# The tail of a one-core transformer block: residual through an identity matmul, W1 over both tiles at once, last copies on two engines

## The chip, the cores and the metric

The kernel runs on one core of one Trainium2 chip. The metric is the device time of one execution in microseconds (us). The engines are PE (TensorE, with its weight load PEld), DVE (VectorE), ACT (ScalarE), POOL (GpSimd) and SP (SyncE, which issues nearly all DMAs). Each works through its own instructions in the order in which the program lists them, and waits for the others through semaphores.

## The reference

One transformer block with adaptive layer norm: 2048 tokens, width 512, 32 heads of 16, an MLP of 1376. The vector c gives six modulation vectors of 512 (sa, ca, ga, sb, cb, gb).

```python
mod = (_silu(c) @ w_mod).reshape(c.shape[0], 6, 1, -1)
sa, ca, ga, sb, cb, gb = (mod[:, 0].copy(), mod[:, 1].copy(), mod[:, 2].copy(),
                          mod[:, 3].copy(), mod[:, 4].copy(), mod[:, 5].copy())
h = _layernorm(x, axis=-1) * (1 + ca) + sa
x = x + ga * _A_ref(h, A_wqkv, A_wo)      # softmax attention, 32 heads of 16, then wo
h = _layernorm(x, axis=-1) * (1 + cb) + sb
x = x + gb * _B_ref(h, B_w1, B_b1, B_w2, B_b2)   # gelu(h @ w1 + b1) @ w2 + b2
```

The gates ga and gb are multiplied into Wo and W2 once, so that a residual is a plain sum.

## The kernel before, in words

The tokens are four blocks of 512 queries (QB); a block is four tiles of 128 tokens (P). A run is one block with four heads: 32 runs, over 16 key tiles each. For a key tile PE computes the transposed scores (L822), an engine takes the exponential, and PE multiplies by V (L960), where one more column of V collects the softmax denominators, into a bank `od`.

The exponential is taken in two ways. ACT takes scores of two or three heads at a time (L871, 128x1024 or 128x1536). Of each run up to four key tiles are offered to DVE (125 in all): it converts scores to integers (L912) and adds four shifts (L927), and PE sums five weighted pieces. ACT takes over such a tile when it has no own one left, so the split follows the order of work.

All other work lies between these: projections, layer norms, and, for each finished block, `block_tail`: W_o and the residual (L1166), layer norm, W1 (L1183), GELU (L1202) and W2 (L1123, L1214).

No engine order is written by hand. The class `Plan` simulates the engines with a fixed cost for every operation while the program is built and always issues the operation that can start first; ties are broken by priorities and by a pseudo-random term, `spread`: SPREAD times a hash of the operation's kind or source line and of one of 32 SEEDS, one for each 25 us. `heat` adds dummy matmuls on PE (L431, L436, L447): PE work within the last WIN = 3.4 us of planned time is summed, and while it is under HEAT, dummy work may go in.

The last block is done in halves, so that its first half (tiles 0 and 1) can be finished under the last attention runs. Its tail, `block_tail(LAST, 2)`, is called after run 27; it loads the whole block's x (512 KB) into `xr`, adds the W_o product of tiles 0 and 1 to it in place (`x2 = xr`), and computes W1 with 256 columns in 11 groups of 128 rows of F. Eight of them (PSUM_F = 8) go through DVE into `g` (L1193), three wait until the attention's banks are free (L1189). GELU needs another ACT table than the exponential, so it and W2 come after the last exponential.

What is left then is `last_half` (L1223 to L1315), tiles 2 and 3. Its steps in before:

- L1226 loads x of the last block a second time. SP issues in order; ahead of it stand the four copies of L1022, which shift the upper half of run 30's product to its place and wait for POOL (L1012).
- L1237 (`early`): W_o over three of the four head groups, which do not need the last run, for both tiles.
- For each tile on DVE: transpose of its half of `od` (L1249), reciprocal of the denominators (L1251), transpose back as a broadcast (L1253), product (L1256). `s` ties the second tile's chain behind the first tile's statistics.
- L1263 (`wo2`): the last head group's W_o, two matmuls. L1267: the residual add on DVE. L1270: statistics; L1271: reciprocal root on POOL; L1272: normalise.
- L1283: four transposes on PE; L1287: modulate, two on DVE and two on ACT.
- L1295: W1 over 128 columns, 44 matmuls for a tile; L1298: GELU, 11 for a tile; L1305 (which prints as L1123): W2, 11 matmuls of 512 columns; L1310: second residual on DVE; L1313: the output DMA.

After the attention, the five banks of the scores become five banks `t` (`r_t`) for these steps; two banks `ax` (`r_ax`) hold W2 of the first half.

Of the kernel before, what the change touches and what calls it, by code (L numbers as in the profile page):

```python
# [11 lines left out]
ACT = mybir.ActivationFunctionType  # L12
ALU = mybir.AluOpType
ENG = mybir.EngineType
BF16 = mybir.dt.bfloat16
FP32 = mybir.dt.float32
# [37 lines left out]
PEL = 0.24  # L54
# [3 lines left out]
DPL = 0.08  # L58
AL = 0.17
FILL = 1.6  # L60
SPREAD = 0.15
SEEDS = (571, 338, 517, 702, 966, 607, 659, 937, 623, 185, 209, 513, 12, 512, 674, 785, 660, 579, 642, 245, 112, 195, 497, 319, 388, 80, 556, 716, 338, 990, 290, 195)
HEAT = 1.3


class Res:
# [191 lines left out]
def kernel(  # L258
# [126 lines left out]
    def op(eng, *a, **k):  # L385
        o = Op(eng, *a, **k)
        if eng == "PE":
            o.due = due_now[0]
            due_now[0] += due_now[1]
        return plan.add(o)  # L390
# [98 lines left out]
    def load_x(b, deps=()):  # L489
        def go(o):  # L490
            nc.sync.dma_start(out=o.tile, in_=x_src[b])
        return dma(go, deps, kb=512, acq=r_xb, prio=0.0)
# [111 lines left out]
    def stats(ln, t, src):  # L604
        mv, _ = ln.tile
        st6 = work.tile([P, 6], FP32, name="ln_s", bufs=2)
        nc.vector.bn_stats(out=st6, in_=src)  # L607
        nc.vector.bn_aggr(out=mv[:, t, :], in_=st6)
# [7 lines left out]
    def apply(ln, z, t, src):  # L616
        mv, rs = ln.tile
        nc.vector.tensor_scalar(out=z.tile[:, t, :], in0=src, scalar1=mv[:, t, 0:1],
                                scalar2=rs[:, t:t + 1], op0=ALU.subtract, op1=ALU.mult)
# [9 lines left out]
    def copy(eng, dst, src):  # L629
        if eng == "ACT":  # L630
            nc.scalar.copy(out=dst, in_=src)
        else:
            nc.vector.tensor_copy(out=dst, in_=src)  # L633
# [480 lines left out]
    def wo_mm(ps, b, t, lo, hi):  # L1114
        for u in range(lo, hi):
            ot, at = (o_OT[(b, (t // 2) * NC + u)], (t % 2) * P) if b == LAST else (o_OT[(b, u)], t * P)
            nc.tensor.matmul(out=ps, lhsT=ot.tile[:, at:at + P], rhs=Wo[:, u, :],
                             start=(u == 0), stop=(u == NC - 1))
# [7 lines left out]
    def rows(f):  # L1126
        return P if f < NF - 1 else FL
# [25 lines left out]
    def block_tail(b, nt=TPB):  # L1153
        kind = "tail"
        due(prog() + 15, (TAIL if b < LAST - 1 else TAIL2 if b < LAST else TAIL3) / (9 * nt - 1))
        N = nt * P
        xr = load_x(b)
        x2 = xr
        ots = [o_OT[(b, u)] for u in range(NC)]
        res_done = []  # L1160
# [62 lines left out]
    def last_half():  # L1223
        r, b = NR - 1, LAST
        full = ("full", 0)
        xr = load_x(b)  # L1226

        def take(acq, deps=()):
            return op("NIL", None, 0.0, deps, lat=0.0, prio=0.0, acq=acq)
        x2 = xr  # L1230
        ln, z, h = take(r_ln, (x2,)), take(r_z, (x2,)), take(r_blk, (x2,))
        g = o_late["part"]
        od, OD, OT = o_od[r], take(r_OD), take(r_OT)
        o_OT[(b, 7)] = OT
        tiles = (2, 3)
        acc = {t: take(r_t) for t in tiles}
        early = {t: op("PE", lambda o, t=t: wo_mm(acc[t].tile, b, t, 0, 3), 3 * MM,  # L1237
                       [acc[t]] + [x for u in range(NC, 7) for x in o_OT[(b, u)].two], lat=PEL, mode=full,
                       kind="last", prio=0.5) for t in tiles}
        s = None  # L1240
        for n, t in enumerate(tiles):
            den = work.tile([P, 8], FP32, name=f"den{t}")

            def half(x, t=t):
                return x.rearrange("p (a q) -> p a q", a=2)[:, :, (t % 2) * P:(t % 2 + 1) * P]

            def turned(n):
                return OD.tile[:, n * HB:(n + 1) * HB].rearrange("p (a q) -> p a q", a=2)
            sh = op("DVE", lambda o, t=t, half=half: nc.vector.transpose(out=turned(0), in_=half(od.tile)), 0.35,  # L1249
                    (o_last[r], OD, s), prio=0.06 + n)  # L1250
            rc = op("DVE", lambda o, den=den: nc.vector.reciprocal(  # L1251
                out=den, in_=OD.tile[:, 16:HB:32]), 0.12, (sh,), prio=0.05 + n)
            bk = op("DVE", lambda o, den=den: nc.vector.transpose(  # L1253
                out=turned(1).rearrange("p a q -> p (a q)"),
                in_=den.unsqueeze(2).to_broadcast([P, 8, 32])), 0.35, (rc,), prio=0.045 + n)
            ml = [op("DVE", lambda o, t=t, half=half: nc.vector.tensor_tensor(  # L1256
                out=half(OT.tile), in0=half(od.tile), in1=turned(1), op=ALU.mult),
                0.36, (bk, OT), prio=0.04 + n)]

            def wo2(o, t=t):  # L1260
                for p in range(2):
                    at = p * HB + (t % 2) * P
                    nc.tensor.matmul(out=acc[t].tile, lhsT=OT.tile[:, at:at + P], rhs=WoP[:, p, :], start=False,  # L1263
                                     stop=(p == 1))
            w = op("PE", wo2, 2 * MM,
                   ml + [early[t]], lat=PEL, mode=full, kind="last", prio=0.2)
            a = op("DVE", lambda o, t=t: nc.vector.tensor_tensor(  # L1267
                out=x2.tile[:, t, :], in0=acc[t].tile, in1=xr.tile[:, t, :], op=ALU.add), 0.62,
                (w, x2, xr), prio=0.024 + n / 50, rel=(acc[t],))
            s = op("DVE", lambda o, t=t: stats(ln, t, x2.tile[:, t, :]), 0.83, (a, ln), prio=0.022 + n / 50)  # L1270
            rs = op("POOL", lambda o, t=t: rstd(ln, t, t + 1), 0.9, (s,), prio=0.0)  # L1271
            za = op("DVE", lambda o, t=t: apply(ln, z, t, x2.tile[:, t, :]), 0.33, (rs, z),  # L1272
                    prio=0.021 + n / 50)

            at = slice((t - 2) * P, (t - 1) * P)
            hd = []
            for e in ("DVE", "ACT"):
                js = (0, 1) if e == "DVE" else (2, 3)

                def tr(o, t=t, js=js):  # L1280
                    o.ps = o.tile.bitcast(BF16)[:, 0:2 * P]
                    for n, j in enumerate(js):
                        nc.tensor.transpose(out=o.ps[:, n * P:(n + 1) * P],  # L1283
                                            in_=z.tile[:, t, j * P:(j + 1) * P], identity=ident)
                tro = op("PE", tr, 2 * 0.0705, (za,), lat=PEL, mode=full, kind="last", acq=r_t, prio=0.1)
                for n, j in enumerate(js):
                    hd.append(op(e, lambda o, n=n, j=j, e=e, at=at, tro=tro: modulate(  # L1287
                        e, h.tile[:, j, at], tro.ps[:, n * P:(n + 1) * P], modB, j), 0.25, (tro, h),
                        prio=0.02, rel=(tro,)))
            gs = slice(HB + (t - 2) * P, HB + (t - 1) * P)  # L1290
            gd = []
            for f in range(NF):
                def w1(o, f=f, at=at):
                    for j in range(NC):
                        nc.tensor.matmul(out=o.tile[:, 0:P], lhsT=W1[:, j, f * P:(f + 1) * P],  # L1295
                                         rhs=h.tile[:, j, at], start=(j == 0), stop=(j == NC - 1))
                mm = op("PE", w1, 4 * 0.071, hd, lat=PEL, mode=full, kind="last", acq=r_t, prio=0.3)
                gd.append(op("ACT", lambda o, f=f, mm=mm, gs=gs: nc.scalar.activation(  # L1298
                    out=g.tile[0:rows(f), f, gs], in_=mm.tile[0:rows(f), 0:P], func=ACT.Gelu_apprx_tanh,
                    bias=b1c[0:rows(f), f:f + 1], scale=1.0), 0.25, (mm,), prio=0.3, rel=(mm,)))  # L1300
            first = prev = None
            for f in range(NF):
                def w2(o, f=f, gs=gs):
                    w2_mm((first_of[id(o)] or o).tile, g.tile, gs.start, f, f + 1)
                o = op("PE", w2, MM, (gd[f], prev), lat=PEL if f == NF - 1 else 0.0, mode=full,  # L1305
                       kind="last", acq=r_t if f == 0 else None, prio=0.4)
                first_of[id(o)] = first
                first = first or o
                prev = o
            a = op("DVE", lambda o, t=t, first=first: nc.vector.tensor_tensor(  # L1310
                out=o.tile, in0=first.tile, in1=x2.tile[:, t, :], op=ALU.add), 0.66, (prev,), prio=0.1,
                acq=r_o, rel=(first,))
            dma(lambda o, t=t, a=a: nc.sync.dma_start(  # L1313
                out=out[0][b * QB + t * P:b * QB + (t + 1) * P, :], in_=a.tile), (a,), kb=128,
                rel=(a,))  # L1315

    first_of = {}

    prev_tr = after = None
    for b in range(NQ):  # L1320
# [132 lines left out]
```

## Time and profile before

| | us |
|---|---|
| median of 12 executions | 789.81 (786.45 to 795.9) |
| profiled execution | 791.02 |
| its span, first to last instruction | 789.2 |
| before the first exponential stretch, 0 to 20 | ACT busy 8.5 |
| attention stage, 20 to 764.6 | ACT busy 737.1, DVE 714.6, PE 704.7 |
| tail, 764.6 to 789.2 | 24.6 long; ACT busy 11.9, DVE 10.4, PE 19.6 |
| VectorE's share of the exponential | 476 score tiles of 128x512 (119 key tiles) |
| dummy matmuls within the attention (L447) | 116, four to a group |
| mean granted TensorE clock | 0.995 |

How to read it: the busy time of a matmul runs from its start to its modelled end, so neighbouring ones overlap, and PE's busy time is more than it can be at its peak. "ACT busy" over a stage says whether the stage is bound by ACT. The granted clock is the share of full speed that the throttle let PE run at; a short dip hardly shows in the mean. Lines of the chain of waits have a start, a length, and the work or queue that the end was waiting for in that stretch.

### The profile page before, as it was taken

What the parts mean: (1) busy time and instruction counts of PE and PEld (TensorE: products, weight loads), DVE (VectorE), ACT (ScalarE), POOL (GpSimd) and SP (SyncE); (2) the same over time, 40 slices, a digit from 0 to 9 for tenths busy, and PEclk for the clock granted to TensorE, in tenths of its full rate; (3) what the DMA queues carried; (4) which work ended last, traced back from release to release, by engine and by line L of the source; (5) the groups of instructions that cost most, each with busy time, mean ns of one, the idle gap of its engine ahead of it and who ended that gap; (6) DMA issues with size and microseconds to landing.
All of it is one profiled execution on the core that took longest, in us unless ns stands there. A gap on an engine that the chain in (4) does not pass through costs nothing.

```text
span 789.2 us, 20525 instructions
## 1 busy us (share of the span) xinstructions
PE 741.1 (94%) x8286; PEld 273.0 (35%) x8286; DVE 737.3 (93%) x1285; ACT 757.6 (96%) x683; POOL 125.4 (16%) x279
## 2 busy tenths in 40 slices
PE   8889999999999898999999999999999999999997
PEld 3433333233332222223232233322243444344454
DVE  6889988999999999999999999999899999999974
ACT  4999999999999999999999999999999999999993
POOL 6511124121134300100002001001000100100100
PEclk9999999999999999999999999999999999999999
DMA  6152001101020010001000110001010001101010
GB/s 214 30 136 89 18 23 46 23 16 22 7 73 22 25 42 23 19 22 28 22 23 18 30 34 21 12 17 32 23 57 21 23 18 33 29 20 28 18 44 28
DMA packets 39073, 28.22 MB, mean 36 GB/s; under 512 B 17957, under 2 KB 34374, under 8 KB 38978
## 3 DMA queue, kind: packets, MB, share of 16 engines
q1 hardware_dynamic: 38970, 26.91, 12.4%
q8 instruction: 65, 1.06, 0.6%
q14 instruction: 30, 0.25, 0.1%
q10 hardware_dynamic: 8, 0.00, 0.0%
HBM read 21.30 MB, written 2.61 MB: 30 GB/s over the span
## 4 chain that ended last, share of the span: by engine, by line
ACT 22%; PE 22%; DVE 12%; issue 7%; DMA 1%; SPq 0%; POOL 0%; POOLq 0%; DVEq 0%; ACTq 0%
ACT pt L871 21%; PE od L960 7%; PE st L822 6%; DVE sh L927 5%; DVE ph L912 4%; PE ax L1123 3%; PE ax L1183 2%; PE ax L822 1%; ACT g L1202 1%; DVE ln_s L607 1%; DVE xb L1166 1%; PE t L1123 1%; DMA xb<-in_A_x_dram 0%; DVE g L1193 0%; DVE OD L985 0%
## 5 line engine op out<-in xcount | busy, mean ns | idle before, releaser
L871 ACT ACTIVATE pt<-st 128x1536 bf16<-128x1536 f32 x629 | 715.7, 1302 | 7.2 <-PE ax L822 3.9
L912 DVE TENSOR_SCALAR ph<-ax 128x512 int16<-128x512 f32 x476 | 311.0, 681 | 13.4 <-PE ax L822 12.1
L927 DVE TENSOR_SCALAR sh<-ph 128x2048 int16<-128x2048 int16 x476 | 311.0, 692 | 2.6 <-PE od L960 2.3
L822 PE MATMUL st<-qm,kT 32*128 32x512 bf16 x1572 | 246.7, 383 | 21.3 <-ACT pt L871 17.2
L822 PE MATMUL ax<-qm,kT 32*128 32x512 bf16 x476 | 167.6, 380 | 8.5 <-DVE ph L912 6.2
L960 PE MATMUL od<-sh,VX 128*32 128x512 bf16 (+1 forms) x2400 | 168.6, 342 | 5.5 <-DVE sh L927 4.5
L822 PEld LDWEIGHTS <-kT 32*128 32x128 bf16 x2048 | 80.5, 91 | 239.3 <-issue 230.3
L960 PE MATMUL od<-pt,VEB 128*32 128x512 bf16 (+1 forms) x1960 | 144.8, 341 | 0.3 <-ACT pt L871 0.3
L960 PEld LDWEIGHTS <-VX 128*32 128x32 bf16 x2400 | 60.7, 95 | 88.3 <-issue 78.0
L960 PEld LDWEIGHTS <-VEB 128*32 128x32 bf16 x2560 | 63.0, 96 | 76.5 <-issue 64.6
L1012 POOL TENSOR_TENSOR OT<-OD,RB 128x256 bf16<-128x256 f32 x38 | 27.3, 729 | 317.3 <-DVE sh L927 200.5
L960 PE MATMUL od<-ph,VEB 128*32 128x512 bf16 (+1 forms) x600 | 48.2, 345 | 1.8 <-DVE OD L985 1.6
L1012 POOL TENSOR_TENSOR OS<-OD,RB 128x256 bf16<-128x256 f32 x24 | 17.2, 729 | 158.1 <-DVE sh L927 110.9
L1183 PE MATMUL ax<-blk,W 128*128 128x512 bf16 (+1 forms) x164 | 41.8, 361 | 0.5 <-DVE ph L912 0.2
L701 PE MATMUL ax<-blk,w 128*128 128x512 bf16 x124 | 36.5, 382 | 2.1 <-DVE blk L626 0.9
L756 POOL TENSOR_SCALAR VX<-VEB 128x128 bf16<-128x128 bf16 x64 | 23.2, 362 | 81.4 <-DVE VEB L633 77.6
L1123 PE MATMUL ax<-w,g 128*128 128x512 bf16 x112 | 30.4, 382 | 0.4 <-DVE ph L912 0.2
L1193 DVE TENSOR_SCALAR g<-ax,b1c 128x512 bf16<-128x512 f32 (+1 forms) x41 | 28.1, 691 | 1.0 <-PE ax L1183 0.7
L607 DVE BATCH_NORM_STATS2 ln_s<-xb 128x6 f32<-128x512 bf16 x32 | 21.6, 675 | 1.5 <-DMA xb<-in_A_x_dram 1.5
L1123 PEld LDWEIGHTS <-g 128*128 128x128 bf16 x176 | 14.0, 97 | 23.3 <-issue 12.7
L985 DVE COPY OD<-od 128x512 f32<-128x512 f32 x31 | 21.1, 680 | 0.9 <-issue 0.5
L1183 PEld LDWEIGHTS <-W 128*128 128x128 bf16 x176 | 14.0, 97 | 20.6 <-issue 14.9
(110 smaller groups left out, 371.2 us busy)
## 6 DMA issues: line engine op xcount, KB each, us to landing
RB<-rn SPq DMA_DIRECT2D x124, 64.0 KB
xb<-in_A_x_dram SPq DMA_DIRECT2D x8, 512.0 KB
out_dram<-o SPq DMA_DIRECT2D x16, 128.0 KB
qm<-qs SPq DMA_DIRECT2D x120, 16.0 KB
W<-in_B_w_dram SPq DMA_DIRECT2D x1, 1376.0 KB
w<-in_A_wqkv_dram SPq DMA_DIRECT2D x3, 384.0 KB
blk<-in_w_mod_dram SPq DMA_DIRECT2D x2, 512.0 KB
xb<-in_w_mod_dram SPq DMA_DIRECT2D x2, 512.0 KB
```

Source lines behind the costliest of these rows:

```text
L607: nc.vector.bn_stats(out=st6, in_=src)
L701: return chain([(lambda ps, j=j: nc.tensor.matmul(out=ps[:, 0:QB], lhsT=w.tile[:, j, cc * P:(cc + 1) * P], rhs=o_h[b].tile[:, j, :], start ...
L756: nc.gpsimd.tensor_scalar(out=v_cols(VX[(t, ph)])[:, 8 * cc:8 * cc + 8, 0:16], in0=v_cols(v_tile(t, 0))[:, 8 * cc:8 * cc + 8, 0:16], scala ...
L822: nc.tensor.matmul(out=o.tile[:, k * QB:(k + 1) * QB], lhsT=kT[cc][kb][rows, ko * P:(ko + 1) * P], rhs=qm.tile[rows, par, :] if hb is None ...
L871: nc.scalar.activation(out=e.tile[:, 0:len(got) * QB], in_=o.tile[:, 0:len(got) * QB], func=ACT.Exp, scale=ESC)
L912: nc.vector.tensor_scalar(out=ph.tile[:, o.row * QB:(o.row + 1) * QB], in0=o.tile, scalar1=PH_B, scalar2=0.0, op0=ALU.add, op1=ALU.max)
L927: sh = op("DVE", lambda o, j=j: nc.vector.tensor_scalar(out=o.tile, in0=first.tile, scalar1=PH_SH[j], scalar2=None, op0=ALU.add), 0.6, es, ...
L960: nc.tensor.matmul(out=o_od[r].tile[32 * i:32 * i + 32, n * HB:n * HB + w], lhsT=v_tile(kt, ph)[:, c0:c0 + 32], rhs=got[i][:, at:at + w], ...
L1012: two = beside(lambda c: nc.gpsimd.tensor_tensor(out=OT.tile[:, c], in0=OD.tile[:, c], in1=o5.tile[:, c], op=ALU.mult), (OT,), (OD, o5))
L1123: nc.tensor.matmul(out=ps, lhsT=g[:, f, col:col + P], rhs=rhs, start=(f == 0), stop=(f == NF - 1))
L1183: mm = chain([(lambda ps, f=f, j=j: nc.tensor.matmul(out=ps[:, 0:N], lhsT=W1[:, j, f * P:(f + 1) * P], rhs=h.tile[:, j, 0:N], start=(j == ...
L1193: ev.append(op("DVE", lambda o, f=f, mm=mm: nc.vector.tensor_scalar(out=g.tile[:, f, 0:N], in0=mm.tile[:, 0:N], scalar1=b1c[:, f:f + 1], s ...
```

## The change

- The tail's second load of x goes; the last block's tail keeps its `xr` for tiles 2 and 3.
- `early` adds x to the W_o bank by an identity matmul. The statistics read the bank; ACT copies it to `x2`; the residual add goes.
- The normalisation of `od` is done once over 512 columns, for both tiles.
- The modulates of both tiles are collected in one list, and W1 runs once over 256 columns, with 11 GELUs of 256 columns.
- W2 of a tile begins with an identity matmul of x2; its end is copied out in two halves, one on DVE and one on ACT.
- HEAT goes from 1.3 to 1.4, SPREAD from 0.15 to 0.06, and all 32 SEEDS are other ones.

```diff
-SPREAD = 0.15
-SEEDS = (571, 338, 517, 702, ...)
-HEAT = 1.3
+SPREAD = 0.06
+SEEDS = (109, 104, 232, 177, ...)
+HEAT = 1.4
...
         xr = load_x(b)
+        if b == LAST:
+            xr.uses += 1
+            o_late["x"] = xr
...
-        xr = load_x(b)
+        xr = o_late["x"]
...
+        def begin(o, t):
+            wo_mm(acc[t].tile, b, t, 0, 3)
+            nc.tensor.matmul(out=acc[t].tile, lhsT=ident, rhs=xr.tile[:, t, :], start=False, stop=False)
+        early = {t: op("PE", lambda o, t=t: begin(o, t), 4 * MM,
+                       [acc[t], xr] + [x for u in range(NC, 7) for x in o_OT[(b, u)].two], lat=PEL, mode=full,
                        kind="last", prio=0.5) for t in tiles}
...
+        sh = op("DVE", lambda o: nc.vector.transpose(out=OD.tile, in_=od.tile), 0.6, (o_last[r], OD), prio=0.06)
+        rc = op("DVE", lambda o: nc.vector.reciprocal(out=den, in_=OD.tile[:, 16:QB:32]), 0.12, (sh,), prio=0.05)
+        bk = op("DVE", lambda o: nc.vector.transpose(
+            out=RB.tile, in_=den.unsqueeze(2).to_broadcast([P, 16, 32])), 0.6, (rc, RB), prio=0.045)
+        ml = [op("DVE", lambda o: nc.vector.tensor_tensor(
+            out=OT.tile, in0=od.tile, in1=RB.tile, op=ALU.mult), 0.62, (bk, OT), prio=0.04)]
+        hd, copies = [], {}
...
-            a = op("DVE", lambda o, t=t: nc.vector.tensor_tensor(
-                out=x2.tile[:, t, :], in0=acc[t].tile, in1=xr.tile[:, t, :], op=ALU.add), 0.62,
-                (w, x2, xr), prio=0.024 + n / 50, rel=(acc[t],))
-            s = op("DVE", lambda o, t=t: stats(ln, t, x2.tile[:, t, :]), 0.83, (a, ln), prio=0.022 + n / 50)
+            s = op("DVE", lambda o, t=t: stats(ln, t, acc[t].tile), 0.86, (w, ln), prio=0.022 + n / 50,
+                   rel=(acc[t],))
+            a = op("ACT", lambda o, t=t: nc.scalar.copy(out=x2.tile[:, t, :], in_=acc[t].tile), 0.5,
+                   (w, x2), lat=0.15, prio=0.02 + n / 50, rel=(acc[t],))
+            copies[t] = a
...
-            za = op("DVE", lambda o, t=t: apply(ln, z, t, x2.tile[:, t, :]), 0.33, (rs, z),
+            za = op("DVE", lambda o, t=t: apply(ln, z, t, x2.tile[:, t, :]), 0.33, (rs, z, a),
...
+        gd = []
+        for f in range(NF):
+            def w1(o, f=f):
+                for j in range(NC):
+                    nc.tensor.matmul(out=o.tile[:, 0:HB], lhsT=W1[:, j, f * P:(f + 1) * P],
+                                     rhs=h.tile[:, j, 0:HB], start=(j == 0), stop=(j == NC - 1))
+            mm = op("PE", w1, 4 * 0.12, hd, lat=PEL, mode=full, kind="last", acq=r_t, prio=0.3)
+            gd.append(op("ACT", lambda o, f=f, mm=mm: nc.scalar.activation(
+                out=g.tile[0:rows(f), f, HB:QB], in_=mm.tile[0:rows(f), 0:HB], func=ACT.Gelu_apprx_tanh,
+                bias=b1c[0:rows(f), f:f + 1], scale=1.0), 0.36, (mm,), prio=0.3, rel=(mm,)))
+        for t in tiles:
...
+            first = op("PE", lambda o, t=t: nc.tensor.matmul(
+                out=o.tile, lhsT=ident, rhs=x2.tile[:, t, :], start=True, stop=False), MM, (copies[t],),
+                mode=full, kind="last", acq=r_t, prio=0.4)
...
-            a = op("DVE", lambda o, t=t, first=first: nc.vector.tensor_tensor(
-                out=o.tile, in0=first.tile, in1=x2.tile[:, t, :], op=ALU.add), 0.66, (prev,), prio=0.1,
-                acq=r_o, rel=(first,))
+            o2 = take(r_o, (gd[NF - 1],))
+            a = [op(e, lambda o, e=e, cs=cs, first=first, o2=o2: copy(e, o2.tile[:, cs], first.tile[:, cs]), us,
+                    (prev, o2), prio=0.1, rel=(first,))
+                 for e, cs, us in (("DVE", slice(0, HB), 0.35), ("ACT", slice(HB, D), 0.32))]
```

## What I predict

> **What bounds the kernel now.** I read the page first, then the windows by stage, the chain of waits over the last 25 us, and last the PE timeline there. The first two say where 97% of the time lies:
>
> ```profile
> L871 ACT ACTIVATE pt<-st 128x1536 bf16<-128x1536 f32 x629 | 715.7, 1302 | 7.2 <-PE ax L822 3.9
> ```
> ```profile
> 20.00:764.60 744.60, 704.70 (x8001) 253.55 (x8001) 714.56 (x1228) 737.10 (x642) 110.55 (x224) 1.00 0.12 31
> ```
>
> The columns of the second are length, then busy time (and count) of PE, PEld, DVE, ACT, POOL, then granted clock. From 20 to 764.6 us ScalarE is busy 737.1 of 744.6 us: the attention stage is bound by the exponentials, and a new order can recover at most 7.5 us of idle ScalarE there, plus work passed to VectorE (30 us idle). Asked in 10 us pieces, two carry 2.7 of the 7.5 us, and 1 us pieces show why:
>
> ```profile
> 130.00:140.00 10.00, 9.86 (x95) 2.64 (x87) 6.84 (x12) 8.76 (x9) 6.09 (x10) 0.84 0.03 7
> ...
> 131.00:132.00 1.00, 1.00 (x12) 0.17 (x4) 0.00 (x0) 0.68 (x1) 1.00 (x2) 0.50 0.00 0
> ...
> 745.00:750.00 5.00, 4.91 (x79) 2.38 (x68) 3.58 (x6) 3.52 (x5) 0.00 (x0) 0.73 0.03 5
> ...
> 746.00:747.00 1.00, 1.00 (x20) 0.36 (x12) 0.17 (x1) 0.00 (x0) 0.00 (x0) 0.50 0.00 0
> ```
>
> The clock falls to 0.50 for about 3.4 us, twice; PE is late with the scores, and ScalarE and VectorE stand. After 764.6 us comes the tail, 24.6 us, where the chain of waits reads (start, length, what):
>
> ```profile
> 766.25 3.94 DMA xb<-in_A_x_dram
> ...
> 770.32 0.70 DVE xb L1267
> ...
> 775.45 0.70 DVE xb L1267
> ...
> 779.83 2.64 PE t L1295 x44
> 782.47 3.25 PE t L1123 x15
> ...
> 785.80 0.69 DVE o L1310
> ```
>
> A late load of x holds the first residual add to 770.32; the second tile's add follows 5.1 us later, as the DVE chain of tile 3 starts only after the statistics of tile 2. But the PE timeline shows what PE does meanwhile:
>
> ```profile
> 768.76 1.46 PE L1123 MATMUL ax<-w,g 128*128 128x512 bf16 x6
> ...
> 770.70 1.67 PE L1123 MATMUL ax<-w,g 128*128 128x512 bf16 x7
> 773.43 0.40 PE L1283 MATMUL t<-ident,z 128*128 128x128 bf16 x4 [1.05 <-DVE z L618]
> ...
> 778.57 0.40 PE L1283 MATMUL t<-ident,z 128*128 128x128 bf16 x4 [0.27 <-DVE z L618]
> ```
>
> It works off W2 of the first half. From 764.95 to 785.53 (start of the last W2 matmul, 785.31, plus one step) it has about 18.6 us of issue time and 1.96 us of holes (0.30 for the GELU at 766.3, 1.23 at 772.2, 0.43 at 778.1). So PE is the tail's real bound, and the DMA wait is mostly hidden.
>
> **What the skill says.** "TensorE: Matmul & The Clock Gate", section "Back-to-back issue gap", prices a step at columns/2.4 + 2.5 ns, 216 ns for 512. The trace agrees: three W2 matmuls take 0.81, less the last one's 0.379, over 2: 0.2155 us; 256 columns 0.110, 128 columns 0.058. The same page, "Part 1: The HAM clock gate", has the array half-clocked after an idle window of about 3.4 us, a window running freely; the trace shows 0.50 for that long, though PE was not idle by its busy row. "VectorE: DVE Perf Modes", section on the TRN2 errata, gives (N+151)/0.96 ns for an fp32 tensor_tensor: 691 at 512 (trace: 692), 424 at 256 (trace: 419). "ScalarE: Activation LUTs", "What ACT_TABLE_LOAD costs", has 280+0.833N ns with a pointer bias and 93 ns of overlap: 400 for 256 columns, where three L1189 GELUs took 1.18 us.
>
> **The change part by part.** Times below run on the profiled execution, 791.02 us, of which the span is 789.2; the median of the runs shown is 1.2 lower, 789.81, and I carry the differences over to it.
>
> *Load.* The second load of x (512 KB, one SP issue, 766.25 to 770.19) goes; tiles 2 and 3 of the load that the block already had (issued at 668.3) are used. Nothing else on SP follows until the outputs at 772.9. Late next is not the load but the W_o product: its third matmul waits for the shifts of run 30 (L1022, issued 763.79 to 766.2), and in before W_o and WoP run 767.01 to 768.75.
>
> *Normalisation over 512 columns, once.* Before, a half took 765.12 to 766.74 (0.45+0.20+0.45+0.42 and gaps). Now two transposes of 512 columns, for which no row exists: between 0.45 (fixed cost dominant) and 0.90 (twice); the 0.96 GHz slope of the errata section adds 0.27, so I take 0.70. With reciprocal 0.20, product 0.69 and four gaps: 2.4, ready at 767.5. That is 0.8 later for tile 2, but covered: WoP cannot issue before 768.3 anyway. With 0.90 it would be 767.9, still covered. Tile 3's own chain (1.45 us of DVE between 771.9 and 774.8) disappears.
>
> *Residual on PE.* Two identity matmuls join the early W_o: +0.43 us. W_o, identity and WoP for both tiles run 767.01 to 769.6. The adds L1267 (0.69 each) go; statistics read PSUM directly (0.69, or up to 0.1 more from PSUM). Two ScalarE copies of 0.63 (as the 128x512 CAST) come in at 769.4, where ScalarE idles 4.89 us; the normalise op waits for them, but they end at 770.7, before the reciprocal roots are there (1.02 after the statistics: 771.3). Nothing else is queued behind them until the modulates.
>
> *One chain for both tiles.* Statistics 769.4 to 770.3 and to 771.2; POOL 0.9 each; normalise 771.3 and 772.25; four transposes each; modulates 0.60 on DVE and 0.81 on ACT per tile, the last at about 774.0. So h of both tiles is complete where before tile 2 alone was (774.5); tile 3's came at 779.6.
>
> *W1 over 256 columns.* 44 matmuls at 0.110 for 88 at 0.058: 4.84 against 5.10, −0.26. GELU: 11 at 0.39 for 22 at 0.265, −1.5 us of ScalarE, which kept up before and does so now (0.39 against PE's 0.44 a group). The added wait for all eight modulates stands at the head of PE's queue; behind it W2 of the first half (22×0.2155 = 4.74) is what PE can do first. It fits: 769.6 + 20×0.2155 + two sets of transposes 0.48 = 774.4.
>
> *Last residual and copies.* Two more identity matmuls, +0.43. L1310 (0.69) becomes half on DVE (0.42) and half on ACT (128x256 without a bias: 0.40 to 0.46): −0.23. The output DMAs are the same, 2.7 us from the last write to the end.
>
> *Sum of the tail.* PE work 18.6 + 0.43 + 0.43 − 0.26 = 19.2, holes 1.96 down to about 0.45: PE ends 764.95 + 19.2 + 0.45 = 784.6 instead of 785.53, −0.9; copies −0.23. Tail: −1.15. No holes at all would give −1.6, today's holes +0.4.
>
> *"Eight early W1 groups".* PSUM_F is 8 in both; no line of the diff changes it. Nothing.
>
> *Constants of the planner.* SPREAD, SEEDS and HEAT reorder the whole program. HEAT 1.4 asks for more PE work in each window before dummy matmuls (29 groups now, L447) stop, so it bears on the two half-clock stretches: ScalarE lost 1.24 + 1.41 = 2.65 us in them. The cost is more filler at 0.2155 a step. If both stretches go, −2.65, with 0.3 given back: −2.3. Bounds: −7.5 (all idle) and, upward, the split of the work: VectorE does 119 tiles (476/4) of the 125 that the code offers it; each tile more on ScalarE costs 4 scores at 0.454 us (59 exponentials in 67.03 us, 2.5 scores each) = 1.82.
>
> **Rivals.**
> *A, forecast:* tail −1.15 and a better-clocked order −2.3: 789.81 − 3.45 = 786.4. For it: the recoverable 2.65 us lie in places that HEAT addresses. Against: 3.4 us windows run freely, so some executions may have lost less.
> *B, tail alone:* the throttled stretches return elsewhere; 789.81 − 1.15 = 788.7. For it: a 0.1 higher target is small.
> *C, slower: the split tips.* With the new order VectorE falls behind by two shared tiles and ScalarE takes them: 2×1.82 − 1.15 = +2.5, 792.3; more tiles, more. It decides from 0.63 of a tile (1.15/1.82) upward. For it: VectorE is at 96% and six tiles already went over; one tile is 5.5 us of VectorE, so coarse. Against: 30 us of idle VectorE.
> *D, W_o late:* run 30's product on POOL (ready long before, held until 762.34 for a place beside VectorE) is placed 1.2 us later; every step of the tail shifts, the tail's gain is gone: 789.8.
>
> **How the numbers follow.** A 0.65, B 0.08, C 0.23, D 0.04. A's own range is 782.5 (most of the idle recovered) to 788.5. The measurement tells 0.3%, 2.4 us, from no change: faster means under 787.4, slower over 792.2. Of A 0.58 lies under 787.4 and 0.07 within; B and D are within (0.12); of C 0.22 lies over. Faster 0.59, same 0.19, slower 0.22. Range: from 782.5 up to 792.8, which takes in C's nearer half; about 0.1 is left out above and below each.
>
> **What would show it.** Right: no xb DMA in the tail, both statistics by 771.5, W1 starting at 774 to 774.5 in one block of 44 at 0.110, PE with under 0.7 us of holes from there on, last copy ended about 1.1 us sooner after the last exponential; granted clock above 0.95 in every 5 us piece of the attention stage and ScalarE idle there near 5 us. Wrong: transposes near 0.9 us and WoP waiting for them; W1 after 775.5; fewer VectorE score evictions than 476 (C), or new half-clock stretches (B).

## The result, and the profile after

The changed kernel takes 794.94 us (median of 12, 791.35 to 799.72) against 788.85 for the kernel before (49 executions): ratio 1.0069, 95% interval 1.0051 to 1.0088. By the ratio it is slower by about 5.4 us; the forecast was 3.4 us faster.

The profiled execution is the shortest: 791.35 us, span 789.6. Time follows the mean granted clock of an execution: 791.35 to 792.91 us at 0.996, 793.49 to 795.04 at 0.991, 799.72 at 0.983. The kernel before has about the same slope but stands elsewhere on it: over all its executions of the experiments below, 785.82 to 788.27 us at a clock of 0.999 or 1.0, and 790.41 to 790.97 at 0.991. No execution of the changed kernel has more than 0.996. So two things are to be explained: what is lost at any clock, and why the clock is never full.

The page of the changed kernel, for the two halves of the exponential (columns: busy, mean ns, idle before and its releaser):

```profile
L871 ACT ACTIVATE pt<-st 128x1536 bf16<-128x1536 f32 x629 | 715.2, 1304 | 8.0 <-PE st L822 5.5
L912 DVE TENSOR_SCALAR ph<-ax 128x512 int16<-128x512 f32 x476 | 312.4, 681 | 14.6 <-PE ax L822 11.1
```

Counts are those of before, 629 and 476: the split of the work did not move. The windows (columns as in the prediction) show that the two stretches at 130 and 745 us are gone:

```profile
130.00:140.00 10.00, 9.73 (x93) 3.06 (x92) 9.87 (x17) 10.00 (x10) 3.74 (x6) 1.00 0.03 8
...
740.00:750.00 10.00, 9.90 (x179) 4.82 (x170) 9.62 (x18) 9.76 (x10) 0.64 (x1) 1.00 0.06 16
```
```profile
580.00:590.00 10.00, 7.69 (x160) 3.86 (x157) 7.93 (x15) 7.96 (x8) 0.00 (x0) 0.95 0.18 52
590.00:600.00 10.00, 10.00 (x126) 3.42 (x122) 8.73 (x15) 8.41 (x8) 0.72 (x2) 0.71 0.11 29
```

They were not fixed features of the old order, though. Of six profiles that have this order in the attention stage (`before` and five of the experiments), four have a half-clock stretch between 125 and 135 us, and only `before` has the one at 745. Instead, ScalarE now loses 3.6 us between 580 and 600, where it lost 1.2 in before. PE's timeline there (start, length, engine, line, what, count, idle before):

```profile
584.83 0.37 PE L822 MATMUL ax<-qm,kT 32*128 32x512 bf16 x1
587.37 0.39 PE L822 MATMUL ax<-qm,kT 32*128 32x512 bf16 x1 [2.17 <-DMA qm<-qs]
```

PE stands for 2.17 us until the queries of run 25 have been copied into `qm` (L729). One-microsecond windows show what the clock does after it:

```profile
586.00:587.00 1.00, 0.00 (x0) 0.00 (x0) 0.00 (x0) 0.22 (x1) 0.00 (x0) 1.00 0.06 13
...
588.00:589.00 1.00, 1.00 (x28) 0.55 (x26) 1.00 (x3) 0.91 (x1) 0.00 (x0) 0.95 0.00 0
589.00:590.00 1.00, 0.86 (x15) 0.37 (x12) 1.00 (x3) 1.00 (x2) 0.00 (x0) 0.50 0.09 8
...
595.00:596.00 1.00, 1.00 (x18) 0.42 (x11) 1.00 (x2) 0.95 (x1) 0.00 (x0) 0.63 0.00 0
```

The clock is at one half from 588.9 to 595.7, 6.8 us. Half of 6.8 us is 0.0043 of the span: this stretch alone brings the mean clock down to 0.996. SP's timeline shows when the copies are issued:

```profile
579.63 3.81 SPq L729 DMA_DIRECT2D qm<-qs  x5
583.53 0.53 SPq L993 DMA_DIRECT2D dc<-dn  x1
584.15 2.37 SPq L729 DMA_DIRECT2D qm<-qs  x3
```

There are eight small DMAs of 0.51 to 1.30 us of issue each, with a step of the previous run's normalisation among them; the last is issued by 586.5, and PE goes on 0.9 us later. The first four runs of the last block need new queries each, the runs of the other blocks only every second one, so here they can be tight. In the kernel before (the first line is of SP) PE waits for copies of the same queries, but less, and five W2 matmuls stand right behind:

```profile
585.26 1.14 SPq L729 DMA_DIRECT2D qm<-qs  x2
...
586.01 0.37 PE L822 MATMUL ax<-qm,kT 32*128 32x512 bf16 x1 [0.80 <-DMA qm<-qs]
586.31 0.82 PE L1123 MATMUL ax<-w,g 128*128 128x512 bf16 x3
586.97 0.59 PE L1123 MATMUL ax<-W2c,g 128*128 128x512 bf16 x2
```

There, too, SP is not done with the copies before 586.40, hardly sooner than in after. The difference is PE's order: its next score matmul starts at 586.01, before SP is done with the last copy, and the W2 matmuls fill the time to the following scores at 587.50. The wait varies from execution to execution: it is 0.80 us in `before`, 0.19 to 1.26 in five other profiles of the old order (none of them with a half-clock stretch right after it), 2.17 in `after` and 2.76 in `order_only` below.

The tail, measured from the start of the GELU's table load (the last exponential is done there) to the end of the span, is 789.6 − 764.08 = 25.5 us; before it was 789.2 − 764.59 = 24.6. In every profile from which a tail is measured here the clock is 1.00 from 757 us to the last matmul. The tail of after is 25.5 in one profile and 25.4 in another (`q_pool`), so differences of 0.2 us say nothing. The chain of waits after:

```profile
765.99 1.71 DMA OT<-OT
...
771.19 0.38 PE t L1299
...
775.52 4.80 PE t L1291 x44
780.32 4.75 PE t L1304 x22
785.07 0.88 PE ax L1123 x4
...
786.03 0.69 DVE o L1217
```

In place of x, the shifts of run 30 now hold W_o. W1 is one block of 44. The last work is not that of tiles 2 and 3 but of the first half's second tile (L1217).

### The profile page after: what moved, and what is told of

Same layout as the page of the kernel before. It is cut to its first block, busy times and chain, and to the rows that moved or that the text cites. A ratio compares the mean times of both kernels' runs of the same rounds, so it can differ in the third digit from the quotient of the medians.

```text
span 789.6 us, 20630 instructions
## 1 busy us (share of the span) xinstructions
PE 739.4 (94%) x8342; PEld 275.3 (35%) x8342; DVE 735.3 (93%) x1279; ACT 757.8 (96%) x676; POOL 126.7 (16%) x279
## 4 chain that ended last, share of the span: by engine, by line
PE 37%; ACT 31%; DVE 19%; issue 10%; DMA 3%; SPq 1%; POOL 0%; DVEq 0%; ACTq 0%; POOLq 0%
ACT pt L871 28%; PE od L960 12%; PE st L822 10%; DVE ph L912 8%; DVE sh L927 7%; PE ax L1123 3%; PE ax L822 2%; PE ax L1186 2%; PE ax L701 2%; DMA dc<-dn 1%; ACT g L1205 1%; DVE OD L985 1%; DVE ln_s L607 1%; PE ax L431 1%; PE t L1291 1%
## 5 line engine op out<-in xcount | busy, mean ns | idle before, releaser
L871 ACT ACTIVATE pt<-st 128x1536 bf16<-128x1536 f32 x629 | 715.2, 1304 | 8.0 <-PE st L822 5.5
L822 PE MATMUL st<-qm,kT 32*128 32x512 bf16 x1572 | 246.9, 384 | 24.1 <-ACT pt L871 19.7
L822 PE MATMUL ax<-qm,kT 32*128 32x512 bf16 x476 | 165.4, 382 | 7.2 <-DMA qm<-qs 2.9
L822 PEld LDWEIGHTS <-kT 32*128 32x128 bf16 x2048 | 80.2, 91 | 236.6 <-issue 223.2
L960 PE MATMUL od<-ph,VEB 128*32 128x512 bf16 (+1 forms) x600 | 46.6, 338 | 1.2 <-DVE OD L985 1.0
L447 PE MATMUL od<-warm 128*32 128x512 bf16 x212 | 20.3, 390 | 0.0
```

Source lines behind the costliest of these rows:

```text
L822: nc.tensor.matmul(out=o.tile[:, k * QB:(k + 1) * QB], lhsT=kT[cc][kb][rows, ko * P:(ko + 1) * P], rhs=qm.tile[rows, par, :] if hb is None ...
L871: nc.scalar.activation(out=e.tile[:, 0:len(got) * QB], in_=o.tile[:, 0:len(got) * QB], func=ACT.Exp, scale=ESC)
L960: nc.tensor.matmul(out=o_od[r].tile[32 * i:32 * i + 32, n * HB:n * HB + w], lhsT=v_tile(kt, ph)[:, c0:c0 + 32], rhs=got[i][:, at:at + w], ...
```

## The experiments

Theory 1: the loss is in the attention stage, made by the new order (SPREAD, SEEDS, HEAT). Theory 2: the tail's own edits make it. A ratio is given against the kernel before, with its 95% interval. "Tail" is the length just defined, read from the one profiled execution of a run.

**The two parts apart.** `tail_only` has the tail's edits with the three constants of before, and keeps the line numbers (the tie-breaking hash uses them). Its diff against after, the constants left out:

```diff
-        xr = load_x(b)
-        if b == LAST:
-            xr.uses += 1
-            o_late["x"] = xr
+        xr = load_x(b); xr.uses += int(b == LAST); o_late["x"] = xr
```

> The tail's edits alone, with SPREAD, SEEDS and HEAT of before; the attention stage has the order of before, instruction by instruction, and only the last 25 us differ. Theory 1 (the time was lost to the new order of the attention stage, by the planner's three constants): within 0.5 us of before, between -0.5 and +1.0 us. Theory 2 (the tail's own edits lost it: copies and statistics of one bank one after the other, the early W_o waiting for the shifts of run 30): +4 to +6 us against before. The forecast's own sum for the tail: -1.15 us.

Measured: 0.9997 (0.998 to 1.0015), 788.73 us; tail 24.6. `order_only` has the three constants of after on the tail of before, three empty lines keeping the line numbers:

> SPREAD, SEEDS and HEAT of after on the tail of before; the attention stage has the order of after, instruction by instruction. Theory 1: +4 to +6 us against before, that is about 793 to 795, with spans that vary from run to run by 5 us or more and follow the mean granted clock (0.996 for the shortest, 0.985 for the longest). Theory 2: within 1 us of before.

Measured: 1.0056 (1.0035 to 1.0077), 793.25 us; clock at most 0.996, as in after, and the same wait, 2.76 us before 588.67. Theory 1 holds, theory 2 falls: the tail's edits together are worth nothing that can be measured, and the order has the loss. Its tail, that of before, is 25.3 us, 0.7 longer than in before's own order; so most of the longer tail of after belongs to the order too (below).

**One constant at a time.**

> HEAT 1.4 on before, all else as before. The forecast's reason (a higher HEAT removes half-clock stretches): mean granted clock 0.997 or more in each run, -1 to -2.5 us. If HEAT works as one more re-draw of the order: anything from -2 to +6 us, with the granted clock and the time moving together, about 1.3 us for each half-clock stretch of 3.4 us (0.002 of the mean clock).

Measured: 1.0139 (1.0097 to 1.0181), 800.13 us, clock 0.987 to 0.994. HEAT 1.4 by itself raises the dummy matmuls of L447 from 116 to 168 and does not raise the clock.

> SPREAD and SEEDS of after with HEAT 1.3 and the tail of before. If the order as such loses the time: +3 us or more against before. If HEAT 1.4 alone loses it (more dummy matmuls in PE's way): within 1 us of before. In both cases some spread of the spans with the granted clock.

Measured: 1.0131 (1.0088 to 1.0174), 800.2 us. Each loses about twice what the constants lose together (six executions of each kernel). Part of that is the split of the exponential, the fear behind the prediction's case C. The page of `heat_only`:

```profile
L912 DVE TENSOR_SCALAR ph<-ax 128x512 int16<-128x512 f32 x464 | 302.4, 681 | 22.6 <-PE ax L822 20.0
```

464 conversions for 476: VectorE did three key tiles fewer, and ScalarE's exponentials (L871) take 722.2 us instead of 715.7. In `seeds_only` it is 468, two tiles, and 719.8 us. The rest of these losses was not taken apart. But PE waits for copies of queries there, too, 0.94 us in two waits up to 596 us in `heat_only` and 1.55 us up to 597 in `seeds_only`, and the clock is at one half right after: 0.66 in the 5 us from 595, and 0.80, 0.50 and 0.67 in the 15 us from 595.

**Is any new draw harmful?** `lines_only` is before with three empty lines ahead of L1156.

> Before with three empty lines put in ahead of L1156 and nothing else: operations defined below get other hashes of their source line, so ties are broken another way from the first block's tail (about 321 us) on. If a new draw of the order costs time by itself, whichever constant draws it (SEEDS fit one exact program): +3 to +12 us, with a mean granted clock of 0.988 to 0.995. If the losses with the single constants came from these constants' values: within 1 us of before.

Measured: 1.0004 (0.9985 to 1.0022). The order changes less than expected: the traces list the same work in the same order until 613 us, and the time does not change; VectorE does 472. A new draw of the last 175 us alone does not cost. Since this leaves the stretch around 585 us as it was, it says nothing of a new draw of the whole program. What a particular order does must be looked up in it.

**The late queries.** If the wait at 585 us is what the order loses, taking it away must bring the time back. `q_pool` leaves the order of PE, VectorE and ScalarE as in after (the traces agree instruction by instruction), and has POOL, idle there, issue half of those eight copies:

```diff
-nc.sync.dma_start(
+(nc.gpsimd if (b, cc) == (LAST, 1) and at.start % 64 >= 32 else nc.sync).dma_start(
```

> After with four of the eight copies of those queries issued by POOL beside SP, so that they land sooner; all compute engines keep their order. If the late queries are what the order of after loses: PE's wait at 585 us shrinks below 1 us, no half-clock stretch follows, and the median is 3 to 4.5 us below after (790.5 to 792). If they are only a part: 1 us or less. POOL's own issue may be slow; then the wait shows it.

Measured: 1.0002 (0.9981 to 1.0024), 789.35 us. The windows of `q_pool`:

```profile
580.00:590.00 10.00, 9.84 (x187) 4.94 (x184) 8.79 (x15) 9.82 (x10) 2.44 (x4) 1.00 0.29 84
590.00:600.00 10.00, 9.42 (x158) 3.92 (x146) 10.00 (x19) 10.00 (x9) 0.50 (x1) 1.00 0.13 29
```

ScalarE is busy 19.8 of these 20 us instead of 16.4, the clock is full, and executions at a clock of 1.0 are back. The late transfer and what follows from it are thus worth 1.0069 − 1.0002 = 0.67%, as much as the whole change lost. That does not make the two orders equal, since before loses time at the same copies (below). `q_fill` separates the two links: it leaves the wait, and puts 11 groups of dummy matmuls ahead of the waiting one:

```diff
-    n_d = [0, 0]
+    n_d = [0, 0]; filled = []
...
-        b = runs[r][0]
+        b = runs[r][0]; r == 25 and not filled and (filled.append(r), [zeros(pv_run[0]) for _ in range(11)])
```

> After with 11 groups of dummy matmuls (2.4 us of PE) put ahead of the first score matmul of run 25, which waits 2.2 us for its queries, unknown to the planner, so that every other engine's order stays. The wait itself stays. If the half-clock stretches at 589 to 596 follow from PE standing still there: the shortest spans now come with a mean clock of 0.999 or more instead of 0.996, and the median is 2 to 3.5 us below after (about 791.5 to 793). If the wait as such is all that costs, or the stretches have another cause: within 1 us of after.

Measured: 1.0046 (1.003 to 1.0061), 792.53 us. PE's timeline of `q_fill`:

```profile
587.04 2.58 PE L447 MATMUL od<-warm 128*32 128x512 bf16 x44
589.55 0.38 PE L822 MATMUL ax<-qm,kT 32*128 32x512 bf16 x1
```

The score matmul is no sooner, rather 0.3 us later (2.82 us after the score before it, 2.54 in after), but the clock reads 1.00 through 598 us. So the half-clock stretch follows from PE's standing still. It costs 1.0069 − 1.0046 = 0.23%, 1.8 us; the larger part, 1.0046 − 1.0002 = 0.44% or 3.5 us, stays with the wait itself, which stops ScalarE for 2.14 us there and VectorE for 2.13. The shares are rough: the intervals of after and `q_fill` overlap, and the dummy matmuls outlast the wait a little. Of the 3.5 us, ScalarE's idle time between 580 and 600 explains 2.1 (2.3 us in `q_fill`, 0.2 in `q_pool`); where the rest goes is open.

**The tail: where its gain went.** `tail_dve_adds` keeps of the tail's edits the dropped load, the single normalisation and W1 over 256 columns, and makes both residuals adds on VectorE again, in the order of before (the part at W2 is left out here):

```diff
-            nc.tensor.matmul(out=acc[t].tile, lhsT=ident, rhs=xr.tile[:, t, :], start=False, stop=False)
...
-            s = op("DVE", lambda o, t=t: stats(ln, t, acc[t].tile), ...)
-            a = op("ACT", lambda o, t=t: nc.scalar.copy(out=x2.tile[:, t, :], in_=acc[t].tile), ...)
+            a = op("DVE", lambda o, t=t: nc.vector.tensor_tensor(
+                out=x2.tile[:, t, :], in0=acc[t].tile, in1=xr.tile[:, t, :], op=ALU.add), ...)
+            s = op("DVE", lambda o, t=t: stats(ln, t, x2.tile[:, t, :]), ...)
```

> The tail's edits without the identity matmuls and without the shared copies: both residuals are adds on VectorE as before; the rest (one normalisation, W1 over 256 columns, no second load of x) as in the tail's edits alone, with the order of before ahead of it. If PE's work bounds the tail, and four identity matmuls (0.86 us) and the hole that they make (0.77 us) ate the gain: the tail from the last exponential to the end is 1.3 to 1.7 us shorter than 24.65 us, and the time about 1.5 us below before (ratio 0.998). If the identity matmuls are worth what they replace: within 0.5 us of before.

Measured: 0.9981 (0.9964 to 0.9998), 787.59 us; tail 785.0 − 761.65 = 23.35, 1.3 us less than `tail_only`. PE's timeline of `tail_dve_adds`:

```profile
765.38 1.03 PE L1256 MATMUL t<-WoP,OT 128*128 128x512 bf16 x4
766.25 1.46 PE L1123 MATMUL ax<-w,g 128*128 128x512 bf16 x6
...
770.77 0.59 PE L1123 MATMUL ax<-W2c,g 128*128 128x512 bf16 x2
771.33 5.25 PE L1287 MATMUL t<-blk,W 128*128 128x256 bf16 x44
```

From W_o on PE has no hole of more than 0.2 us, and all of the first half's W2 is done before W1 starts. In after the same stretch has holes (PE, then VectorE, then ScalarE of after):

```profile
767.83 0.38 PE L1117 MATMUL t<-Wo,OT 128*128 128x512 bf16 x1 [0.74 <-DMA OT<-OT]
...
771.19 0.38 PE L1299 MATMUL t<-xb,ident 128*128 128x512 bf16 x1 [0.61 <-ACT xb L1266]
...
785.12 0.81 PE L1123 MATMUL ax<-W2c,g 128*128 128x512 bf16 x3
```
```profile
769.82 0.70 DVE L607 BATCH_NORM_STATS2 ln_s<-t 128x6 f32<-128x512 f32 x1 [2.66 <-PE t L1260]
...
771.66 0.70 DVE L607 BATCH_NORM_STATS2 ln_s<-t 128x6 f32<-128x512 f32 x1 [0.92 <-ACT xb L1266]
...
785.11 0.42 DVE L633 CAST o<-t 128x256 bf16<-128x256 f32 x1 [1.95 <-PE t L1304]
786.03 0.69 DVE L1217 TENSOR_TENSOR o<-ax,xb 128x512 bf16<-128x512 f32 x1 [0.49 <-ACT o L631]
```
```profile
770.56 1.07 ACT L1266 CAST xb<-t 128x512 bf16<-128x512 f32 x2 [2.10 <-DVE ln_s L607]
...
785.57 0.37 ACT L631 CAST o<-t 128x256 bf16<-128x256 f32 x1 [2.00 <-DVE o L633]
```

In each place where ScalarE and VectorE read one PSUM bank, they do it one after the other: the copy of tile 2 starts 0.04 after its statistics end, tile 3's statistics start when both copies are over, and of the two halves of the last copy the second starts when the first ends (785.53, 785.57). The Trainium skill, "PSUM — Partial Sum Buffer", section "Terms", says that two engines on the same bank and quadrant (32 partitions) at once collide, reads against reads included; the program orders such reads by waits, and the trace shows the waits, not what would happen without them. The planner knew nothing of this: it thought the copies done at once, queued the final identity matmul (L1299) right behind them, and PE stood 0.61 us in front of it. `tail_stats_first` tells the planner:

```diff
-                   (w, x2), lat=0.15, prio=0.02 + n / 50, rel=(acc[t],))
+                   (w, x2, s), lat=0.15, prio=0.02 + n / 50, rel=(acc[t],))
```

> The tail's edits alone, with the ScalarE copies put behind the statistics of the same bank by the planner too. If PE's hole of 0.77 us came from the final identity matmul queued ahead of a copy that really starts only when the statistics have left the bank: the hole goes, the second statistics start some 1 us earlier, and the tail from the last exponential's end to the end is 0.5 to 0.9 us shorter than 24.65. If PE is full anyway: within 0.2 us of 24.65. (Tail lengths from the profile; one time cannot tell this.)

Measured, in one execution: tail 787.7 − 763.75 = 23.95, 0.7 us shorter than `tail_only`. Of its VectorE timeline:

```profile
768.62 0.70 DVE L607 BATCH_NORM_STATS2 ln_s<-t 128x6 f32<-128x512 f32 x1 [1.78 <-PE t L1257]
769.35 0.18 DVE L608 BATCH_NORM_AGGREGATE mv<-ln_s 128x2 f32<-128x6 f32 x1
769.45 0.67 DVE L607 BATCH_NORM_STATS2 ln_s<-t 128x6 f32<-128x512 f32 x1
```

The second statistics now come right after the first. About half of the 1.3 us by which `tail_only` is longer than `tail_dve_adds` was this hole; the other half is left for the identity matmuls' own time and the copies in sequence, which were not taken apart. `load_only` takes away just the second load from before:

> Before without the second load of x, nothing else. If PE bounds the tail and the DMA wait was hidden: the tail shrinks from 24.63 by 0.3 to 1.2 us, the holes on PE, though the first residual add starts 1.5 us sooner (at about 4.2 us after the last exponential's end instead of 5.7). If the DMA wait was on the path: by 1.5 us.

Measured, in one execution: tail 784.7 − 760.65 = 24.05, 0.55 us shorter than before. The first residual add starts at 765.09, 4.4 us after the table load's start instead of 5.7: 1.3 us sooner, of which 0.55 reach the end. The load was mostly hidden.

**Both repairs together.**

> The tail with adds on VectorE (0.9981 of before) and the order of before, with four of the eight query copies of run 25 issued by POOL. Before waits 0.8 us for the same copies. If late queries cost here too: another 0.5 to 1.3 us, ratio about 0.997, about 786.6. If the W2 matmuls that stand in that wait in the order of before cover it: no more than tail_dve_adds, ratio 0.998.

Measured: 0.9965 (0.9952 to 0.9978), 787.02 us: the best of all, 2.8 us below before by the ratio. ScalarE is busy 9.92 of 580 to 590 us, against 9.56 in `tail_dve_adds` and 8.83 in before: the order of before lost time to the same copies, if not in every execution as much.

> After with both repairs: query copies shared with POOL, both residuals as adds on VectorE. If the two losses are separate and these are all: 1.0002 - 0.0016, ratio 0.998 to 0.999 (787.5 to 788.2). If the adds bring less because the shifts of run 30 land late in this order: 0.9995 to 1.0005.

Measured: 0.9991 (0.997 to 1.0012), 788.84 us; tail 24.1. These two kernels differ in the order alone, and that of after is the slower one by 0.9991/0.9965 = 1.0026, about 2 us; the intervals hardly meet. At a clock of 1.0 the one takes 786.3 and 786.97 us, the other 784.25 to 786.08. The order cost 0.56% by `order_only`, and 0.72% by after against `tail_only`. So the late queries are half to two thirds of what the order lost, not all. Some 0.8 to 1.0 us of the rest are in the tail (24.1 against 23.35 in `tail_dve_adds` and 23.1 in `dve_adds_q_pool`). In after, POOL's product for run 30 ends at 764.1, as the last exponential does; in before it ends 0.8 us earlier than that. W_o's wait of 0.74 us for its shifts, in `order_only` as in after, fits this. About 1 us is not located.

## Why the prediction was wrong

The forecast was −3.4 us, the result +5.4. By its steps:

- **What bounds the kernel.** Right: ScalarE in the attention stage, PE in the tail.
- **Load.** Right: hidden but for 0.55 us. The shifts of run 30 are late next, as it said, in the new order alone (0.74 us); in `tail_only` W_o does not wait for them.
- **Normalisation over 512 columns.** Right: the transposes took 0.72 and 0.71 (0.70 taken), the chain 3.1 us after the last exponential (2.9).
- **Residual on PE.** Wrong. The copies were set beside the statistics, ending before the reciprocal roots; they run after them in the same bank. Counted from the last exponential's end, the second statistics began in `tail_only` after 6.7 us, not 5.7, and h was complete after 10.6, not 9.4; PE had 0.6 us of hole ahead of the identity matmul. (In after it was 11.4, since the new order also starts the first statistics 0.9 us later.) Undoing this step and the last copies together gave 1.3 us (`tail_dve_adds`).
- **W1 over 256 columns.** Right: 4.97 us with the last one's drain (4.84 of issue), one block, ScalarE keeping up.
- **Last copies.** Wrong, the same error: half and half was to save 0.23, and took 0.42 + 0.37 one after the other, 0.83 from 785.11 to 785.94 against 0.69. The very last output was the first half's, since the planner put its last four W2 matmuls behind everything, and the add behind them ended the tail.
- **Sum of the tail.** −1.15 forecast, 0.0 measured for the edits (`tail_only`), +0.9 in the profile with the new order. Case D's mechanism came true there, at 0.7 of its 1.2 us.
- **Constants of the planner.** This is the step that failed and decided. The prediction let the higher HEAT bear on the two half-clock stretches and set −2.3 us for both gone. It counted what a new order could recover, and, apart from the split of case C, put at nothing, without a reason, what the old order protected. The measured order cost +4.4 us (`order_only`). The two stretches were gone, but another, of 6.8 us, came after a wait of 2.2 us that had been 0.8. HEAT by itself did not raise the clock. The recoverable time was also too large: it came from one execution of 791.02 us, and 24 of the 127 executions of before in the experiments have a clock of 0.999 or 1.0, so hardly any such stretch to win back. The list of PE's waits in before had this one, `PE ax L822 <- DMA qm<-qs: 0.8, 1, 0.8`, among many of its size, and it was given no part in the forecast.
- **Case C** (slower) named the side, with a price of 792.3, but not the cause: after's split is unchanged at 476. Its mechanism is real in `heat_only` and `seeds_only`.
- **Two small slips.** The shown line gives a loss of 1.48 us, not 1.41, for ScalarE in the second stretch; and 0.01 of case C's chance was counted under faster. Neither bears on the outcome.

The bounds of this step were open upward only by case C, so the range ended at 792.8, 2.1 us short.

Not settled: what else differs between the two orders. With the late queries mended in both, that of after is still about 2 us slower, half of it in the tail. Nor is it known why `heat_only` and `seeds_only` lose more than their split of the exponential explains.

## What to carry to other kernels

When a change re-orders a whole program, list in the old profile the short waits of the bounding engines that other work happens to fill, and price each as if its filling were gone, with the clock that follows. Read the gain from more than one execution, too: a half-clock stretch that one of them has, another of the same kernel may not have. A tuned set of order constants belongs to one program: test it against the change without it before crediting either. Sharing the reading of a PSUM bank between two engines bought nothing here, where their reads are ordered one after the other, and a planner that does not know it queues other engines behind the mistake.

## What the runs showed of the hardware

- PE still for 2.2 us was enough for the clock to fall to 0.50, from 1.5 us after work resumed, and for 6.8 us; with dummy matmuls in the gap it did not fall. In `order_only`, after 2.8 us of standing, it fell for 10.2 us (the clock is 0.84, 0.50 and 0.64 in the three 5 us windows from 585). With the 3.4 us of the stretches in before, these are one, two and three times the same length.
- Time against granted clock within one kernel: in before 11 us from a clock of 1.0 (786.2) to 0.982 (797.3). One stretch of 3.4 us at half clock is 1.7/789 = 0.0022 of the mean, so by these two ends about 1.3 us each, an estimate.
- Eight copies of 16 KB within SBUF need 5 to 6 us of issue on SP's queue; four of them on POOL took 2.44 us, about as long as four on SP in before (2.41).
